# The value products of an attention kernel, as one product of 128 keys or as two of 64 on the two halves of TensorE's rows

## The chip, the cores and the metric

The kernel runs on one core of one Trainium2 chip. The metric is the device time of one execution in microseconds (us), lower is better. Engines are named as in the profile: PE is TensorE's matrix products, PEld its weight loads, DVE is VectorE, ACT ScalarE, POOL GpSimd, SP the engine that issues the transfers.

## What is computed

A layer norm, then an attention block with 32 heads of only 16 elements each, beside a gated feed-forward block that reads the same normalised input. All of it is float32.

```
x = A_x                                   # 1 x 2048 x 512
xn = layernorm(x)
q, k, v = split(xn @ A_wqkv)              # 32 heads of 16
p = softmax(q @ k^T / 4)                  # 2048 x 2048 for each head
s = (p @ v) @ A_wo
gate, up = xn @ B_w1, xn @ B_w3           # 512 -> 1792
g = silu((silu(gate) * up) @ B_w2)        # 1792 -> 512
return x + s * g
```

## The kernel before

**Stages.** A prologue of about 160 us normalises and transposes the input and makes queries, keys and values. Then comes one long stretch, to about 1625 us of the profile, in which attention and the feed-forward block run interleaved on PE. A tail of some 120 us multiplies by the output weights.

**Attention.** It works on pairs of heads. A phase is one pair of heads and one half of the 2048 queries, 32 phases in all. Four kinds of work on PE belong to the long stretch:

- `m` (line 389, `max_unit`): scores of 128 queries against 512 keys, of which DVE takes the row maxima (line 391). The maxima of the next phase are made during the present one. 2048 in all.
- `e` (line 626, `scores`): the scores again, keys on the output's partitions, of which ACT takes the exponential (line 629) into a tile `pt` of 128 keys x 512 queries. 2048 in all.
- `pv` (line 639, `values`): four exponentiated tiles times the values of their 128 keys, with a column of ones that adds up the softmax's denominator. Each of the four is a product with 17 output columns that stands on its own group of 32 columns of the array, so the four stand side by side. 512 such groups, 16 for each phase, and all 16 of a phase add up in one PSUM bank, `pv`. Operands are float32, and the hardware carries out each such product as two instructions.
- `f` (line 857, `Lanes.emit`): the products of the feed-forward block, each matrix product as three of rounded parts.

**Halves of the rows.** `m`, `e` and `f` have at most 64 rows of weights. Each stands on rows 0 to 63 of the array (lane 0) or on rows 64 to 127 (lane 1), and two of different lanes run at the same time. A `pv` product of before needs all 128 rows.

**PSUM.** Of eight banks one is `pv`. The other seven are handed out one by one by `take`, to whichever of `m`, `e`, `f` asks next. A bank that went to an `m` is free again when DVE has read it, that of an `e` when ACT has. A product of the `f` kind holds its bank while 12 to 24 instructions of each lane add up in it; two such products can be open at once, one to a lane.

**The order.** A table of letters, `ORDER_OF_ISSUE`, sets what PE gets next: small letters are lane 0, capitals lane 1, `s` stands for an `e` product, `v` for a group of value products, `r` for one behind the transposition of new maxima. An entry for which the program's own clock (`Model`) sees no bank or no input yet is put off and tried again at each later entry. The letters are counted here as they come out in the built program. There are 380 places with one or more `v` in a row, 512 groups in all. In the long stretch 214 of the ways from one such place to the next have 12 other entries or fewer; they hold 287 groups and 610 `m`. The other 141 ways are longer, 46 entries on the average; they hold 189 groups, 1331 `m` and 1333 `e`, which together are 41% of their entries.

**Taking out.** At the end of a phase `take_out` has ACT copy the bank `pv` to SBUF (line 645), and the first `pv` product of the next phase waits for that copy. Sums of exponentials then go through DRAM to become reciprocals on all partitions, and POOL multiplies. The ring of `pt` tiles has 23 buffers (`PTS`); an `e` of a new group is let out only while fewer than that are owed.

Of the kernel before, what the change touches and what calls it, by code (L numbers as in the profile page):

```python
# [9 lines left out]
F32 = mybir.dt.float32  # L10
# [7 lines left out]
P = 128  # L18
S, D, F = 2048, 512, 1792
# [19 lines left out]
AHEAD = 5  # L39
HALF = P // 2  # L40
# [105 lines left out]
def kernel(ctx: ExitStack, tc: tile.TileContext, x, wqkv, wo, w1, w3, w2, out):  # L146
# [11 lines left out]
    BANKS = 7  # L158
# [16 lines left out]
    pv = psum.tile([P, 512], F32, tag="pv", name="pv", bufs=1)  # L175
# [242 lines left out]
    with tc.tile_pool(name="pro", bufs=1) as pro, tc.tile_pool(name="pros", bufs=1) as pros:  # L418
# [121 lines left out]
        nc.vector.memset(pv, 0.0)  # L540
# [93 lines left out]
    def values(p, half, k, pts):  # L634

        last = (p, half) == LAST
        for j, pt in enumerate(pts):
            key = k * 2 % NT + j // 2 if last else k
            nc.tensor.matmul(pv[32 * j:32 * j + VW, :], vt[2 * p // GH][:, key, 2 * p % GH + j % 2, :], pt,  # L639
                             start=key < 2 if last else k == 0, stop=key >= NT - 2 if last else k == NT - 1)  # L640

    def take_out(p, half):

        ot = work.tile([P, 512], F32, tag="ot", name="ot", bufs=2)
        nc.scalar.copy(ot, pv)
# [395 lines left out]
    def pt_tile(dtype):  # L1041
        return work.tile([P, 512], dtype, tag="pt", name="pt", bufs=PTS)
# [5 lines left out]
    def projecting():  # L1048

        if not steps or min(free_at) > mod.now + EARLY or not can(*steps[0][:2]):  # L1050
            return False
        what, b, t = steps.pop(0)
# [49 lines left out]
    count = {"S": 0, "M": 64, "V": 0, "chunks": 0, "phase": 1}  # L1102
# [90 lines left out]

    def issue_v():
# [4 lines left out]
        values(p, half, k, [c["pts"][j] for j in range(4)])  # L1199
# [7 lines left out]
        if k == NT - 1 and j < PHASES - 3:  # L1207
            g = take_out(p, half)
            next(g)
            outs.append([mod.now + 2.0, g, j, -1])  # L1210
        elif k == (NT - 1 if j < PHASES - 1 else NT // 2 - 1) and j >= PHASES - 3:
            sums[j] = [work.tile([P, 512], F32, tag="ot", name="ot", bufs=2)]
            nc.scalar.copy(sums[j][0], pv)
        else:
            return
        pv_free = mod.work("act", begins + mod.VALUES + 0.3, 0.6) + mod.NOTICE
# [3 lines left out]
    def half_issued(what, h):  # L1220

        if what == "f":
# [64 lines left out]

    ot, oh, ol = pt_tile(F32), pt_tile(F32R), pt_tile(F32R)
    nc.scalar.copy(ot, pv)
# [51 lines left out]
```

## Time and profile before

| | |
|---|---|
| time, two runs | 1749.95 and 1750.27 us, median 1750.11 |
| span of the profiled execution | 1747.2 us, first to last instruction |
| granted TensorE clock | 1.000 |
| PE, PEld busy | 1737.2, 1027.4 us |
| DVE, ACT, POOL busy | 1432.9, 1258.9, 764.1 us |

The profile is of one execution; its own time is known by its span, and the runs' median is 2.9 us more than that. Instruction lines such as L639 are lines of the kernel before. In the changed kernel the same statements stand a little lower: `m` at L391, its maximum at L393, `e` at L629, `pv` at L643, `f` at L867. The PE time of a row counts from an instruction's start to its modelled end, so products that follow each other at full rate overlap in it.

### The profile page before, as it was taken

The page shows a single profiled execution, that of the slowest core. Times are in us where ns is not written, and L with a number is a line of the kernel's source. Part 1 is how long each engine was busy: PE and PEld are TensorE (multiplying, and loading weights), DVE is VectorE, ACT ScalarE, POOL GpSimd, SP SyncE. Part 2 cuts the span into 40 slices and gives each one's busy share as a digit, 9 for nine tenths or more (in the row PEclk, how much of TensorE's full clock was granted, in tenths as well). Part 3 has the DMA queues.
Part 4 walks back from the last instruction along what each step waited for, and adds up shares of the span by engine and source line. Part 5 has one row for each costly group of instructions (what it writes and reads, how often), then busy time and mean ns, then how long its engine had stood idle before and what let it go on. Part 6 is the DMA issues. An engine that isn't in the chain of part 4 may idle for free.

```text
span 1747.2 us, 35524 instructions
## 1 busy us (share of the span) xinstructions
PE 1737.2 (99%) x13188; PEld 1027.4 (59%) x13188; DVE 1432.9 (82%) x2343; ACT 1258.9 (72%) x2440; POOL 764.1 (44%) x791
## 2 busy tenths in 40 slices
PE   9999999999999999999999999999999999999998
PEld 7876655555555555555555565565555565555455
DVE  7576988888888888898888888898888897898625
ACT  4223788778878787778778877788787867868861
POOL 3102744346526561546356452555265615562101
PEclk9999999999999999999999999999999999999999
DMA  8657213132323222231433231132322321331542
GB/s 286 239 200 206 59 41 71 47 71 54 80 76 85 65 56 50 62 81 47 93 98 68 51 80 29 50 68 75 101 80 62 81 39 55 101 93 31 172 155 97
DMA packets 146798, 155.37 MB, mean 89 GB/s; under 512 B 42304, under 2 KB 100672, under 8 KB 143648
## 3 DMA queue, kind: packets, MB, share of 16 engines
q1 hardware_dynamic: 145760, 151.52, 32.0%
q8 instruction: 104, 1.70, 0.4%
q10 hardware_dynamic: 864, 1.57, 0.2%
q14 instruction: 70, 0.57, 0.1%
HBM read 107.97 MB, written 44.02 MB: 87 GB/s over the span
## 4 chain that ended last, share of the span: by engine, by line
PE 92%; issue 4%; DMA 2%; SPq 1%; DVE 0%; ACT 0%; POOL 0%; ACTq 0%; POOLq 0%
PE f L857 27%; PE pv L639 26%; PE e L626 17%; PE m L389 14%; PE m L507 2%; PE e L195 2%; PE e L199 2%; PE e L197 2%; PE m L480 0%; PE m L404 0%; DMA ovl<-o 0%; DMA wl<-g 0%; SPq L894 0%; DMA inh<-in_A_x_dram 0%; DMA last<-in_A_wo_dram 0%
## 5 line engine op out<-in xcount | busy, mean ns | idle before, releaser
L391 DVE TENSOR_REDUCE mp<-m 128x1 f32<-128x512 f32 x2048 | 1301.3, 684 | 192.2 <-PE m L389 123.8
L629 ACT ACTIVATE pt<-e 128x512 f32<-128x512 f32 x2048 | 1091.3, 605 | 301.9 <-PE m L389 130.7
L626 PE MATMUL e<-qs,ks 64*128 64x512 f32 x2048 | 713.2, 413 | 1.8 <-DMA qs<-ml 1.8
L389 PE MATMUL m<-ks,qs 62*128 62x512 f32 x2048 | 691.9, 411 | 0.2 <-DVE mp L391 0.2
L639 PE MATMUL pv<-pt,vt 128*17 128x512 f32 x4096 | 515.0, 597 | 0.0
L626 PEld LDWEIGHTS e<-qs,ks 64*128 64x128 f32 x2048 | 340.1, 184 | 266.8 <-ACT pt L629 87.9
L389 PEld LDWEIGHTS m<-ks,qs 62*128 62x128 f32 x2048 | 337.1, 184 | 123.3 <-ACT pt L629 39.6
L639 PEld LDWEIGHTS pv<-pt,vt 128*17 128x17 f32 x4096 | 81.1, 96 | 202.6 <-issue 194.3
L857 PE MATMUL f<-xtl,wh 64*128 64x512 f32 x488 | 171.8, 391 | 0.0
L857 PE MATMUL f<-xth,wl 64*128 64x512 f32 x488 | 171.7, 396 | 0.0
L857 PE MATMUL f<-xth,wh 64*128 64x512 f32 x488 | 169.0, 392 | 0.0
L742 POOL TENSOR_TENSOR h<-g,h 128x512 f32<-128x512 f32 x56 | 71.9, 1284 | 215.9 <-ACT h L738 215.8
L857 PE MATMUL f<-wh,hs 64*128 64x512 f32 x496 | 148.4, 395 | 0.0
L857 PE MATMUL f<-xth,xel 64*128 64x512 f32 x408 | 147.4, 396 | 0.0
L857 PE MATMUL f<-xth,xeh 64*128 64x512 f32 x408 | 144.7, 393 | 0.0
L857 PE MATMUL f<-xtl,xeh 64*128 64x512 f32 x408 | 143.9, 392 | 0.0
L322 POOL TENSOR_TENSOR wl<-wr,wh 128x512 fp32r<-128x512 f32 x92 | 118.4, 1287 | 7.7
L857 PE MATMUL f<-xeh,hs 64*128 64x512 f32 x400 | 121.5, 393 | 0.0
L321 POOL TENSOR_SCALAR wh<-wr 128x512 fp32r<-128x512 f32 x92 | 56.9, 619 | 115.1 <-PE m L389 47.7
L322 POOL TENSOR_TENSOR xel<-wr,xeh 128x512 fp32r<-128x512 f32 x76 | 97.9, 1288 | 6.3
L726 POOL TENSOR_SCALAR th<-th 128x512 f32<-128x512 f32 x56 | 34.6, 618 | 133.2 <-ACT th L719 133.2
L857 PEld LDWEIGHTS f<-xtl,wh 64*128 64x128 f32 x488 | 85.9, 185 | 6.8
(179 smaller groups left out, 2027.4 us busy)
## 6 DMA issues: line engine op xcount, KB each, us to landing
wr<-in_B_w_dram SPq DMA_DIRECT2D x168, 256.0 KB
qs<-qk SPq DMA_DIRECT2D x186, 64.0 KB
ks<-qk SPq DMA_DIRECT2D x90, 128.0 KB
qk<-sh SPq DMA_DIRECT2D x32, 256.0 KB
qk<-sl SPq DMA_DIRECT2D x32, 256.0 KB
v<-vrow SPq DMA_DIRECT2D x16, 272.0 KB
xin<-in_A_x_dram SPq DMA_DIRECT2D x16, 256.0 KB
g<-part SPq DMA_DIRECT2D x16, 256.0 KB
```

The source lines that it names most:

```text
L195: nc.tensor.matmul(ps, lhs[1], rhs[0], start=first, stop=False)
L197: nc.tensor.matmul(ps, lhs[0], rhs[1], start=False, stop=False)
L199: nc.tensor.matmul(ps, lhs[0], rhs[0], start=False, stop=last)
L321: nc.gpsimd.tensor_scalar(hi, t, 1.0, 1.0, op0=ALU.mult, op1=ALU.mult)
L322: nc.gpsimd.tensor_sub(lo, t, raw(hi))
L389: nc.tensor.matmul(ps, qs[p % 2][64 * h:64 * h + KM, q0:q0 + P], ks[p % 2][64 * h:64 * h + KM, c * 512:(c + 1) * 512], start=True, stop=True)
L391: nc.vector.reduce_max(mp[p, half][:, h, qt, c:c + 1], ps, axis=AX.X)
L626: nc.tensor.matmul(ps, ks[p % 2][64 * h:64 * h + KR, k * P:(k + 1) * P], qs[p % 2][64 * h:64 * h + KR, q0:q0 + 512], start=True, stop=True)
L629: nc.scalar.activation(pt, ps, AF.Exp, scale=DH ** -0.5)
L639: nc.tensor.matmul(pv[32 * j:32 * j + VW, :], vt[2 * p // GH][:, key, 2 * p % GH + j % 2, :], pt, start=key < 2 if last else k == 0, stop= ...
L742: nc.gpsimd.tensor_mul(h2, g, h2)
L857: nc.tensor.matmul(ps, left[r], right[r], start=starts and lane == 0, stop=ends and lane == 1)
```

## The change

- `values` gets a lane. The keys of a `pt` tile are halved: the first 64 are multiplied on lane 0 and add up in one PSUM bank, the last 64 on lane 1 and add up in a second bank. Instead of four products of 128 rows x 17 columns there are twice four of 64 rows x 17 columns.
- The first half is issued where the group was issued before. The second half is put in a list and issued `SHIFT = 6` entries of the table later, or earlier where a next group, the end of a phase (or half of the last one), or an output product comes first.
- There are now two `pv` banks and six instead of seven for everything else.
- Taking out (`taken`) is ACT's copy of the first bank and an addition of the second on DVE; `Model` books DVE's share too.
- A new exponential is let out by the count of second halves issued (`W`), not of first ones.

In the built program 186 of the 512 groups have the two halves next to each other; in the other 326 entries lie between, five of them in 305 cases.

```diff
+SHIFT = 6
...
-    BANKS = 7
+    BANKS = 6
...
-    pv = psum.tile([P, 512], F32, tag="pv", name="pv", bufs=1)
+    pvs = [psum.tile([P, 512], F32, tag=f"pv{h}", name="pv", bufs=1) for h in range(2)]
+    pv = pvs[0]
...
-    def values(p, half, k, pts):
+    def values(p, half, k, pts, lane):
 
         last = (p, half) == LAST
+        r = slice(HALF * lane, HALF * lane + HALF)
         for j, pt in enumerate(pts):
             key = k * 2 % NT + j // 2 if last else k
-            nc.tensor.matmul(pv[32 * j:32 * j + VW, :], vt[2 * p // GH][:, key, 2 * p % GH + j % 2, :], pt,
-                             start=key < 2 if last else k == 0, stop=key >= NT - 2 if last else k == NT - 1)
+            nc.tensor.matmul(pvs[lane][32 * j:32 * j + VW, :], vt[2 * p // GH][r, key, 2 * p % GH + j % 2, :],
+                             pt[r], start=key < 2 if last else k == 0,
+                             stop=key >= NT - 2 if last else k == NT - 1)
+
+    def taken(ot):
+
+        nc.scalar.copy(ot, pvs[0])
+        nc.vector.tensor_add(ot, ot, pvs[1])
...
-        if 4 * count["V"] + PTS <= count["S"]:
+        if 4 * count["W"] + PTS <= count["S"]:
...
+    halves = []
+
+    def second_half(now=True):
+
+        for e in list(halves):
+            e[0] -= 1
+            if now or e[0] <= 0:
+                halves.remove(e)
+                values(*e[1:], 1)
+                count["W"] += 1
+
     def issue_v():
...
-        values(p, half, k, [c["pts"][j] for j in range(4)])
+        second_half()
+        pts = [c["pts"][j] for j in range(4)]
+        values(p, half, k, pts, 0)
+        halves.append([SHIFT, p, half, k, pts])
+        if k in (NT - 1, NT // 2 - 1):
+            second_half()
...
-        pv_free = mod.work("act", begins + mod.VALUES + 0.3, 0.6) + mod.NOTICE
+        pv_free = mod.work("dve", mod.work("act", begins + mod.VALUES + 0.3, 0.6), 0.6) + mod.NOTICE
...
     def half_issued(what, h):
 
+        second_half(False)
```

**PE, at a place where one group follows another closely** (near 541.5 us of the profile; `pt` numbers name the exponentiated tiles, pv_65 is the first bank, pv_66 the second). Before:

```order
L389 MATMUL m_7617<-ks0_134,qs0_132 128x512
L626 MATMUL e_7620<-qs1_133,ks1_135 128x512
L639 MATMUL pv_65<-pt_7519,vt_1710 17x512
L639 MATMUL pv_65<-pt_7563,vt_1710 17x512
L639 MATMUL pv_65<-pt_7527,vt_1710 17x512
L639 MATMUL pv_65<-pt_7573,vt_1710 17x512
L626 MATMUL e_7631<-qs1_133,ks1_135 128x512
L389 MATMUL m_7635<-ks0_134,qs0_132 128x512
L626 MATMUL e_7642<-qs1_133,ks1_135 128x512
L389 MATMUL m_7646<-ks0_134,qs0_132 128x512
L626 MATMUL e_7649<-qs1_133,ks1_135 128x512
L626 MATMUL e_7653<-qs1_133,ks1_135 128x512
```

The same place in the changed kernel:

```order
L643 MATMUL pv_65<-pt_8008,vt_1712 17x512
L643 MATMUL pv_65<-pt_8062,vt_1712 17x512
L629 MATMUL e_8124<-qs1_134,ks1_136 128x512
L391 MATMUL m_8128<-ks0_135,qs0_133 128x512
L629 MATMUL e_8131<-qs1_134,ks1_136 128x512
L391 MATMUL m_8135<-ks0_135,qs0_133 128x512
L629 MATMUL e_8138<-qs1_134,ks1_136 128x512
L643 MATMUL pv_66<-pt_8000,vt_1712 17x512
L643 MATMUL pv_66<-pt_8052,vt_1712 17x512
L643 MATMUL pv_66<-pt_8008,vt_1712 17x512
L643 MATMUL pv_66<-pt_8062,vt_1712 17x512
L629 MATMUL e_8146<-qs1_134,ks1_136 128x512
```

The four products became four on the first half (two of them shown) and four of the same tiles on the second half, behind five entries. The five, `SmSmS` in the table's letters, are the same as before and in the same order: lanes 1, 0, 1, 0, 1.

**PE, away from the value products** (near 1307.6 us). The `f` with wl5 and wh5 and the `e` behind them are lane 0; the `f` with wl4 and wh4 behind that `e` are lane 1. Before:

```order
L857 MATMUL f_19392<-xth_18481,xeh_1564 128x512
L857 MATMUL f_19642<-xth_18481,wl5_19023 128x512
L857 MATMUL f_19642<-xtl_18482,wh5_19022 128x512
L626 MATMUL e_19645<-qs1_133,ks1_135 128x512
L857 MATMUL f_19557<-xth_18481,wl4_19019 128x512
L857 MATMUL f_19557<-xtl_18482,wh4_19018 128x512
L389 MATMUL m_19651<-ks0_134,qs0_132 128x512
```

In the changed kernel:

```order
L867 MATMUL f_20897<-xth_19921,xeh_1566 128x512
L867 MATMUL f_21167<-xth_19921,wl5_20495 128x512
L867 MATMUL f_21167<-xtl_19922,wh5_20494 128x512
L867 MATMUL f_21078<-xth_19921,wl4_20491 128x512
L867 MATMUL f_21078<-xtl_19922,wh4_20490 128x512
L629 MATMUL e_21172<-qs1_134,ks1_136 128x512
L391 MATMUL m_21176<-ks0_135,qs0_133 128x512
```

Only a neighbour's place moved here (the `e` went behind two `f`): away from the groups the change reaches the order through the number of banks alone.

**DVE, around the end of a phase** (the maxima are L391 before and L393 after). Before:

```order
L408 TENSOR_TENSOR ml<-m,mh 16x128
L391 TENSOR_REDUCE mp<-m 128x1 x43
L653 RECIPROCAL rec<-sums 128x16
L391 TENSOR_REDUCE mp<-m 128x1 x13
L397 TENSOR_REDUCE mx<-mp 128x16
```

In the changed kernel:

```order
L410 TENSOR_TENSOR ml<-m,mh 16x128
L393 TENSOR_REDUCE mp<-m 128x1 x18
L650 TENSOR_TENSOR ot<-ot,pv 128x512
L393 TENSOR_REDUCE mp<-m 128x1 x23
L663 RECIPROCAL rec<-sums 128x16
L393 TENSOR_REDUCE mp<-m 128x1 x15
```

The addition of the second bank stands in the row of maxima, 18 of them behind the row `ml`; the maxima behind it wait until ACT's copy and the addition are done.

More of the change, by code (lines that the diff above doesn't have):

```diff
@@ L539 @@
             run(products)
-        nc.vector.memset(pv, 0.0)
+        for t in pvs:
+            nc.vector.memset(t, 0.0)
         for n in range(2):
@@ L1101 @@
     opened, closed = [], []
-    count = {"S": 0, "M": 64, "V": 0, "chunks": 0, "phase": 1}
+    count = {"S": 0, "M": 64, "V": 0, "W": 0, "chunks": 0, "phase": 1}
     keys = {0: 0.0, 1: 0.0}
@@ L1212, in issue_v @@
             sums[j] = [work.tile([P, 512], F32, tag="ot", name="ot", bufs=2)]
-            nc.scalar.copy(sums[j][0], pv)
+            taken(sums[j][0])
         else:
             return
-        pv_free = mod.work("act", begins + mod.VALUES + 0.3, 0.6) + mod.NOTICE
+        pv_free = mod.work("dve", mod.work("act", begins + mod.VALUES + 0.3, 0.6), 0.6) + mod.NOTICE
         if j in sums:
@@ L1286 @@
                 mod.wait(0.1)
+    second_half()
     ot, oh, ol = pt_tile(F32), pt_tile(F32R), pt_tile(F32R)
-    nc.scalar.copy(ot, pv)
+    taken(ot)
     def whole(adder):
```

3 lines of the change are left out of this document (2 added, 1 removed).

## The prediction, as put on record before the result

> **What bounds the kernel now.** I read the page's first parts, then the long stretch as a window, then the timeline around one group of value products, then two places that show when the array has to run empty.
>
> ```profile
> span 1747.2 us, 35524 instructions
> PE 1737.2 (99%) x13188; PEld 1027.4 (59%) x13188; DVE 1432.9 (82%) x2343; ACT 1258.9 (72%) x2440; POOL 764.1 (44%) x791
> ...
> PE f L857 27%; PE pv L639 26%; PE e L626 17%; PE m L389 14%; PE m L507 2%; PE e L195 2%; PE e L199 2%; PE e L197 2%; PE m L480 0%; PE m L404 0%; DMA ovl<-o 0%; DMA wl<-g 0%; SPq L894 0%; DMA inh<-in_A_x_dram 0%; DMA last<-in_A_wo_dram 0%
> ...
> L391 DVE TENSOR_REDUCE mp<-m 128x1 f32<-128x512 f32 x2048 | 1301.3, 684 | 192.2 <-PE m L389 123.8
> L629 ACT ACTIVATE pt<-e 128x512 f32<-128x512 f32 x2048 | 1091.3, 605 | 301.9 <-PE m L389 130.7
> ```
>
> ```profile
> 160.00:1625.00 1465.00, 1462.95 (x11782) 841.44 (x11784) 1269.05 (x2063) 1148.59 (x2218) 720.36 (x737) 1.00 0.28 69
> ```
>
> PE is busy 99% of the span and is 92% of the chain of waits, a quarter of it in the value products. In the window of the long stretch (columns: length, then busy PE, PEld, DVE, ACT, POOL) PE fills 1463 of 1465 us, but DVE has 1269 and ACT 1149. So PE is the bound, with DVE 13% behind it. A busy PE is not a full array, though, and the timeline of all engines at one group shows where it isn't:
>
> ```profile
> 541.45 0.39 PE L626 MATMUL e<-qs,ks 64*128 64x512 f32 x1
> 541.76 0.13 PEld L639 LDWEIGHTS pv<-pt,vt 128*17 128x17 f32 x8 [0.36 <-issue]
> 541.77 1.05 PE L639 MATMUL pv<-pt,vt 128*17 128x512 f32 x8
> 542.75 0.18 PEld L626 LDWEIGHTS e<-qs,ks 64*128 64x128 f32 x1 [0.85 <-ACT pt L629]
> 542.75 0.49 PE L626 MATMUL e<-qs,ks 64*128 64x512 f32 x1
> 542.75 0.49 PE L389 MATMUL m<-ks,qs 62*128 62x512 f32 x1
> 543.08 0.39 PE L626 MATMUL e<-qs,ks 64*128 64x512 f32 x1
> 543.28 2.06 ACT L629 ACTIVATE pt<-e 128x512 f32<-128x512 f32 x4 [0.69 <-PE m L389]
> 543.31 0.39 PE L626 MATMUL e<-qs,ks 64*128 64x512 f32 x2
> 543.31 1.29 DVE L391 TENSOR_REDUCE mp<-m 128x1 f32<-128x512 f32 x2 [0.26 <-PE m L389]
> 543.64 1.05 PE L639 MATMUL pv<-pt,vt 128*17 128x512 f32 x8
> ```
>
> The chain of waits gives a group's length:
>
> ```profile
> 1453.55 1.84 PE pv L639 x16
> ...
> 1462.74 0.99 PE pv L639 x8
> ```
>
> One more group costs 1.84 - 0.99 = 0.85 us. From 543.08 to 543.31 a pair of entries takes 0.23. The last `e` before the group starts at 541.45, so its lane is free at 541.68, but the group starts at 541.77: 0.09 lost. The group's 0.85 ends at 542.62, the next pair starts at 542.75: 0.13 lost. The pair after that comes 0.33 later instead of 0.23: 0.10 lost. Together **0.32 us around each place with value products**, and the group's weights (541.76) are loaded only as it starts.
>
> **Does the change remove that?** It does if a change of the number of columns needs no emptying, and if the lanes run on independently. For the first, PE alone where products of 128 rows meet products of 62, all of 128 columns:
>
> ```profile
> 106.43 0.39 PE L199 MATMUL e<-xeh,wqh 128*128 128x512 f32 x1
> 106.75 0.73 PE L389 MATMUL m<-ks,qs 62*128 62x512 f32 x4
> 107.41 0.50 PE L507 MATMUL m<-wqh,xel 128*128 128x512 f32 x1
> 107.75 0.39 PE L507 MATMUL m<-wql,xeh 128*128 128x512 f32 x1
> ```
>
> and the timeline where 128 columns turn to 16 at unchanged 128 rows:
>
> ```profile
> 154.83 0.39 PE L199 MATMUL e<-xth,wqh 128*128 128x512 f32 x1
> 154.83 0.09 PEld L404 LDWEIGHTS m<-ident,nm 128*16 128x16 f32 x1
> 155.06 0.27 PE L404 MATMUL m<-ident,nm 128*16 128x128 f32 x1
> 155.06 0.19 PEld L195 LDWEIGHTS e<-xth,wql 128*128 128x128 f32 x1
> 155.08 0.47 PE L195 MATMUL e<-xth,wql 128*128 128x512 f32 x1
> ```
>
> In the first, 0.32 (106.43 to 106.75) and 0.34 (107.41 to 107.75) stand in place of 0.23: the row halving alone costs what the groups cost. In the second, the weights of 16 columns load under the product before (154.83), and their product starts 0.23 later, at full rate. So I read the loss as one of the row division; the changed groups keep to the 64 rows of their neighbours. The Trainium skill ("TensorEngine Tiling (Array Packing)", Key Properties) says that changing the tiling mode drains TensorE, and counts 64x128 and 64x32 as different modes; the trace agrees for rows and not for columns at 128 rows, and has no row for columns at 64.
>
> For the second, PE at a place where the order of issue (shown with the change) has a lane-0 `e` ahead of two lane-1 `f` with wl and wh:
>
> ```profile
> 1307.58 0.60 PE L857 MATMUL f<-xth,wl 64*128 64x512 f32 x2
> 1307.89 0.53 PE L857 MATMUL f<-xtl,wh 64*128 64x512 f32 x2
> 1308.12 0.39 PE L626 MATMUL e<-qs,ks 64*128 64x512 f32 x1
> ```
>
> All four `f`, those two included, have started before the `e`. A lane does pass instructions of the other that are stuck. In the trace it passes two or three; a changed group leaves eight and more.
>
> **The sum, against the span of 1747.2.** In the changed kernel each half group takes its lane 0.85 us, so a lane's work is what it was, and with 2.5 slots of 0.23 between the halves the lanes stay level.
>
> 1. *Losses around the groups*: 380 places x 0.32 = -122 us. Ends: nothing (no overlap), and all of it.
> 2. *DVE in the close groups.* From 541.77 to 543.64, 1.87 us, stand a group and six entries, three of them maxima. On PE they would take 0.85 + 3 x 0.23 = 1.54. DVE needs (row of two maxima: 1.29 - 0.68 = 0.61 apart) 3 x 0.61 = 1.83. So here 0.04 is saved instead of 0.32. Taking the larger of the two needs for each of the 214 short ways, by their letters in the order of issue, about half of 214 x 0.32 = 68 us stays: +35.
> 3. *A bank fewer.* An `e` and an `m` start at 542.75; ACT begins at 543.28 and takes 0.60, DVE begins at 543.31 and takes 0.68, so a bank is held 1.13 to 1.24 us, 1.2 on the average, where nothing queues. While two `f` products are open, `m` and `e` have five banks of seven now, and four of six then: at most 4 / 1.2 = 3.3 a microsecond instead of 4.2. On the long ways they are 41% of the entries, two entries per 0.23 us: 3.6 a microsecond between groups, and 18.9 per way. 18.9 / 3.3 = 5.7 us is under the 6.35 that PE would take (1.34 groups x 0.85 + 22.7 pairs x 0.23), but not always evenly spread. Ends: 0, and all of the 141 x 0.32 = 45 or more (third rival). I take half: +22.
> 4. *Taking out*: 32 additions on DVE of about 0.6 us = +19 at most, where DVE is what PE waits for. DVE then waits for ACT's copy with maxima queued behind it, and the first group's second half of the next phase waits for the addition; six entries cover that (0.7 us). I count 19; ends 0 and 32 x 1.3 = 42, if ACT's 0.6 is uncovered too.
> 5. *At nothing*: 4096 more instructions on PE, with as many loads (eight loads take 0.13 us at 541.76, under the other lane's work; uncovered 512 x 0.13 = 67); `pt` tiles released up to a microsecond later (the ring of 23 holds nearly six groups; uncovered, ACT waits that microsecond at some groups); the reciprocal's transfers a DVE step later, with entries of the next phase over them; no transfer is issued in another place, so the queues of SP and POOL change only with what releases them. The prologue is as before, PE bound at 128 rows.
>
> -122 + 35 + 22 + 19 = -46: a span of 1701, and with the 2.9 us between span and median **1704**; for entries that wait a little for each other at 326 split groups (0.01 each) I say 1708. That is 2.4% less. About 2% either way, 35 us, is what a measurement of this kernel can tell from no change.
>
> **The rivals.**
>
> *All of it arrives.* Banks and additions stay hidden: 1747 - 122 + 35 = 1660, 1663 as a time; without DVE's share too 1628. For it speaks that no wait for a bank is seen outside the 0.85 of a group. Against it: DVE at 1269 + 19 in about 1360 us would be 95% busy.
>
> *The queue blocks (slower).* If an entry of lane 0 behind the first half holds up lane 1 behind it, a split group takes 0.85 + 2.5 x 0.23 + 0.85, less 0.23 beside the second half and 0.12 beside the first (a capital leads in half the cases) = 1.93, where 0.85 + 0.32 + 0.58 = 1.75 stood: 326 x 0.18 = +59; the some 55 places without a split save 18; with the additions 1747 + 59 - 18 + 19 = 1807, **1810**. It decides where fewer than about eight stuck instructions can be passed. The Trainium skill ("TensorE: Matmul & The Clock Gate", What overlaps and what doesn't) has matmuls start in strict program order; at 1307.89 to 1308.12 the trace differs.
>
> *The array empties for columns too, so the change doesn't do what it says.* Each split group then has two turns of 0.85 + 0.32 instead of one: 326 x 1.17 = +381, 2147 with the additions, **2150**. Against it are the rows at 154.83 to 155.08. By the skill's rule on modes, above, this is what would happen.
>
> *Banks become the bound (slower).* On the long ways four banks and 18.9 results in 6.69 us (1.34 x 0.85 + 0.32 + 22.7 x 0.23) break even at a hold of 4 x 6.69 / 18.9 = 1.42 us; at 1.24 they don't bind. If entries that start under a half group hold their bank for its 0.85 us, some three of 18.9, the mean is 1.2 + 3 x 0.85 / 18.9 = 1.33; with a queue of 0.2 on DVE it is 1.5, a way takes 7.1, and 141 x 0.4 = 56 us are lost: 1747 + 56 + 19 = 1822, **1825**, or near 1750 at 1.42.
>
> **The numbers.** My forecast, 1708, has a chance of 0.42, with a range of its own of 1675 to 1750; 0.27 of that lies below 1715. All of it arriving: 0.17. Banks binding: 0.20, half of it within 2%. The blocked queue: 0.13, nearly all slower. The emptied array: 0.08. So faster by over 2%: 0.27 + 0.17 = 0.44; slower: 0.10 + 0.12 + 0.08 = 0.30; within: 0.26. A range of 1640 to 1825 leaves out the emptied array and the ends of the others.
>
> **What would show it.** Right: `pv` rows of 64 x 17 with other rows' products starting inside their 0.85 us; a weight load for them ahead of their start; the next entry of the other lane 0.23 behind its predecessor. DVE's share of the long stretch rises to some 93%. Wrong: no product of lane 1 starts within a first half (blocked or emptied; emptied if 0.09 and more is lost at each end of every half); waits of PEld on ACT and DVE outside the groups, with PE rows apart (banks). Step 2 is wrong if close groups come every 1.6 us, step 4 if DVE idles 1 us ahead of each L650.

## The result and the profile after

The changed kernel takes 2308.41 us (two runs, 2306.80 and 2310.03) where the kernel before takes 1750.11: 1.3194 times as long (95% interval 1.3155 to 1.3232), 558 us slower. The prediction was 1708 with a range of 1640 to 1825. The profiled execution after has a span of 2305.0 us, 557.8 more than before, at a granted clock of 0.997.

Parts of the page of the changed kernel (span, PE, the chain of waits by line, and two groups of instructions):

```profile
span 2305.0 us, 43733 instructions
...
PE 2286.0 (99%) x17284; PEld 1107.5 (48%) x17284; DVE 1481.3 (64%) x2377; ACT 1307.2 (57%) x2440; POOL 763.1 (33%) x791
...
PE pv L643 33%; PE f L867 21%; PE e L629 18%; PE m L391 15%; PE m L509 2%; ACT pt L632 1%; PE e L197 1%; PE e L201 1%; PE e L199 1%; DVE mp L393 1%; PE m L406 0%; DMA qk<-sl 0%; PE m L482 0%; DMA inh<-in_A_x_dram 0%; PE pv L452 0%
...
L393 DVE TENSOR_REDUCE mp<-m 128x1 f32<-128x512 f32 x2048 | 1328.2, 686 | 639.0 <-PE m L391 431.3
L643 PE MATMUL pv<-pt,vt 64*17 64x512 f32 x8192 | 840.3, 595 | 0.0
```

PE still counts as busy for 99% of the span, although it does the same work in 558 us more: a time in which one lane works and the other stands still counts in full. What shows the loss is the other side: DVE's maxima have hardly grown (1301 to 1328 us), but DVE stood idle ahead of them for 639 us where it was 192, most of it for PE, and the value products' share of the chain went from 26% to 33%.

The window of the long stretch of the changed kernel (length, then busy PE, PEld, DVE, ACT, POOL):

```profile
160.00:2180.00 2020.00, 2008.35 (x15712) 922.87 (x15710) 1324.86 (x2110) 1205.53 (x2235) 722.35 (x740) 1.00 0.21 51
```

It answers to 1465 us before, with about the same work of DVE, ACT and POOL in it. DVE's share fell from 87% to 66%; the prediction had it rise to 93%.

The timeline around two groups of the changed kernel, PE and its weight loads:

```profile
699.68 0.39 PE L867 MATMUL f<-xth,xel 64*128 64x512 f32 x1
699.68 0.63 PE L391 MATMUL m<-ks,qs 62*128 62x512 f32 x2
...
700.24 0.13 PEld L643 LDWEIGHTS pv<-pt,vt 64*17 64x17 f32 x8 [0.37 <-issue]
700.24 1.05 PE L643 MATMUL pv<-pt,vt 64*17 64x512 f32 x8
701.22 0.18 PEld L867 LDWEIGHTS f<-xtl,xeh 64*128 64x128 f32 x1 [0.85 <-issue]
701.22 0.50 PE L867 MATMUL f<-xtl,xeh 64*128 64x512 f32 x1
...
701.23 0.73 PE L391 MATMUL m<-ks,qs 62*128 62x512 f32 x2
...
701.89 1.93 PE L643 MATMUL pv<-pt,vt 64*17 64x512 f32 x32
...
703.75 0.49 PE L391 MATMUL m<-ks,qs 62*128 62x512 f32 x1
```

The eight instructions at 700.24 are one half of a group, on one lane. They load their weights only as they start, no product of the other lane begins beside them, and the next loads and products begin together 0.98 us later. Before, a whole group took 0.98 from its start to the next product's (541.77 to 542.75). So **half a group alone costs what a whole group cost**. The 32 instructions at 701.89 are two groups with their halves side by side: 1.86 us, about as much as two groups before (1.84).

Cutting the long stretch, in both traces, at each start of value products and at each next start of another product (160 us to the last `f`; the sums are worked out from PE's starts, the entries of each lane are counted in the built program, and 0.205 is what is lost ahead of a place and in the second pair behind it):

| part of the long stretch, us | before | after | more |
|---|---|---|---|
| places with value products (361; 655) | 453.6 | 744.5 | 291 |
| ends of the stretches between: 0.205 x 355 and 649 | 73 | 133 | 60 |
| the fuller lane of each stretch, entries x 0.227 | 895 | 961 | 66 |
| what is left of the stretches: waits | 28 | 150 | 122 |

That is 539 us; the other 19 lie in the tail. The first three lines belong together: the array runs empty at 655 places instead of 361, and with five entries between two halves one lane has three of them and the other two. The fourth, the waits, is another thing.

### The profile page after: what moved, and what is told of

Read it like the earlier page. It is cut to its first block, busy times and chain, and to the rows that moved or that the text cites. A ratio compares the mean times of both kernels' runs of the same rounds, so it can differ in the third digit from the quotient of the medians.

```text
span 2305.0 us, 43733 instructions
## 1 busy us (share of the span) xinstructions
PE 2286.0 (99%) x17284; PEld 1107.5 (48%) x17284; DVE 1481.3 (64%) x2377; ACT 1307.2 (57%) x2440; POOL 763.1 (33%) x791
## 4 chain that ended last, share of the span: by engine, by line
PE 92%; issue 4%; ACT 1%; DVE 1%; SPq 1%; DMA 1%; POOL 0%; ACTq 0%; POOLq 0%; DVEq 0%
PE pv L643 33%; PE f L867 21%; PE e L629 18%; PE m L391 15%; PE m L509 2%; ACT pt L632 1%; PE e L197 1%; PE e L201 1%; PE e L199 1%; DVE mp L393 1%; PE m L406 0%; DMA qk<-sl 0%; PE m L482 0%; DMA inh<-in_A_x_dram 0%; PE pv L452 0%
## 5 line engine op out<-in xcount | busy, mean ns | idle before, releaser
L393 DVE TENSOR_REDUCE mp<-m 128x1 f32<-128x512 f32 x2048 | 1328.2, 686 | 639.0 <-PE m L391 431.3
L632 ACT ACTIVATE pt<-e 128x512 f32<-128x512 f32 x2048 | 1133.7, 598 | 762.1 <-PE e L629 390.5
L643 PE MATMUL pv<-pt,vt 64*17 64x512 f32 x8192 | 840.3, 595 | 0.0
L629 PE MATMUL e<-qs,ks 64*128 64x512 f32 x2048 | 789.0, 440 | 5.7 <-ACT pt L632 2.4
L391 PE MATMUL m<-ks,qs 62*128 62x512 f32 x2048 | 766.5, 433 | 5.4 <-ACT pt L632 3.6
L391 PEld LDWEIGHTS m<-ks,qs 62*128 62x128 f32 x2048 | 343.4, 185 | 269.1 <-ACT pt L632 109.1
L643 PEld LDWEIGHTS pv<-pt,vt 64*17 64x17 f32 x8192 | 124.5, 92 | 286.7 <-issue 280.1
L867 PE MATMUL f<-xtl,wh 64*128 64x512 f32 x488 | 184.8, 413 | 0.0
L867 PE MATMUL f<-xth,wl 64*128 64x512 f32 x488 | 183.9, 411 | 0.0
L867 PE MATMUL f<-xth,wh 64*128 64x512 f32 x488 | 180.7, 407 | 0.0
L867 PE MATMUL f<-wh,hs 64*128 64x512 f32 x496 | 160.1, 408 | 0.5 <-ACT pt L632 0.5
```

Source lines behind the costliest of these rows:

```text
L391: nc.tensor.matmul(ps, qs[p % 2][64 * h:64 * h + KM, q0:q0 + P], ks[p % 2][64 * h:64 * h + KM, c * 512:(c + 1) * 512], start=True, stop=True)
L393: nc.vector.reduce_max(mp[p, half][:, h, qt, c:c + 1], ps, axis=AX.X)
L629: nc.tensor.matmul(ps, ks[p % 2][64 * h:64 * h + KR, k * P:(k + 1) * P], qs[p % 2][64 * h:64 * h + KR, q0:q0 + 512], start=True, stop=True)
L632: nc.scalar.activation(pt, ps, AF.Exp, scale=DH ** -0.5)
L643: nc.tensor.matmul(pvs[lane][32 * j:32 * j + VW, :], vt[2 * p // GH][r, key, 2 * p % GH + j % 2, :], pt[r], start=key < 2 if last else k == 0,
L867: nc.tensor.matmul(ps, left[r], right[r], start=starts and lane == 0, stop=ends and lane == 1)
```

## The experiments

Times stand against the kernel before, timed beside each of them (medians 1749.9 to 1750.3), with the ratio and its 95% interval where a kernel was timed more than once.

**What makes the array run empty.** Products of constants, one kind at a time, in a row of six pairs of rounded products of 64 rows x 128 columns:

```
for _ in range(4):
    c = bank("c", "lowA")
    nc.tensor.matmul(c[0:17], w[low, 0:17], m[low], start=True, stop=True)
    lanes("afterA")
```

> This kernel leaves out the whole computation: it runs matrix products of constants on PE alone, four times each, and the output is a constant. Between six pairs of products of 64 rows x 128 columns (the two halves of the rows) one product on lane 0 is put: A four-byte float of 17 columns at column 0, B the same at column 32, C of rounded type with 16 columns, D four-byte float of 128 columns, E rounded with 64, F rounded with 100, G the four groups of 17 side by side. Then the same among products of 128 rows: H rounded with 16 columns, I float with 17, J float with 128, K a transposition to 16 columns, L float with 17 at column 32. Theory 'columns empty the array': A, B and G start only when both lanes are done, some 0.1 us late, their weights are loaded as they start, and the next pair starts 0.1 us and more behind their end; D has its weights loaded ahead and the other lane goes on beside it; C, E and F tell from how few columns on it happens (C as A). Among 128 rows H, I and L lose 0.2 to 0.3 us each and K nothing, since a transposition is not split by columns. Theory 'the type empties the array' (four-byte float among rounded): A, B, D, G, I, J, L lose, C, E, F, H do not. Theory of the prediction, rows alone: nothing in A to L loses 0.1 us.

> As the first run of single products, nothing of the layer is computed: among pairs of rounded products of 64 rows x 128 columns one product is put on lane 0, four times each: four-byte float with A 16, B 32, C 64, D 100 columns; rounded with E 128 and F 32 columns; G four-byte float with 17 columns on both lanes; H rounded with 16 columns on both lanes. What a product adds to its six pairs (6 x 0.2275) is compared with its own time (0.85 us float, 0.23 rounded). In the first run it was 0.33 more for float with 17 columns, at 64 and at 128 rows, 0.11 more for rounded with 16 to 100 columns, 0.02 more for float with 128. Theory 'columns and type together': A to C lose 0.33, D 0.1 or less, E nothing, F 0.11, G 0.33 once for both, H 0.11. Theory 'one product on one lane costs 0.11 of evenness whatever its shape, and only 32 columns or fewer empty the array': E 0.11 too, H nothing, C and D as E, A and B 0.33.

The timeline of the first of these kernels at a float product of 17 columns (lowA, one product on lane 0):

```profile
20.12 0.39 PE L41 MATMUL afterA<-mr,wr 64*128 64x512 f32 x1
20.13 0.39 PE L42 MATMUL afterA<-mr,wr 64*128 64x512 f32 x1
20.44 0.11 PEld L52 LDWEIGHTS lowA<-m,w 64*17 64x17 f32 x2 [0.36 <-issue]
20.44 1.03 PE L52 MATMUL lowA<-m,w 64*17 64x512 f32 x2
21.40 0.18 PEld L41 LDWEIGHTS afterA<-mr,wr 64*128 64x128 f32 x1 [0.85 <-PE afterA L42]
21.40 0.49 PE L41 MATMUL afterA<-mr,wr 64*128 64x512 f32 x1
```

PE alone in the second kernel, at a float product of 64 columns (lowC) and at one of 100 (lowD):

```profile
40.24 0.39 PE L41 MATMUL afterC<-mr,wr 64*128 64x512 f32 x1
40.57 1.07 PE L60 MATMUL lowC<-m,w 64*64 64x512 f32 x2
41.57 0.50 PE L41 MATMUL afterC<-mr,wr 64*128 64x512 f32 x1
...
48.00 0.39 PE L42 MATMUL afterC<-mr,wr 64*128 64x512 f32 x1
48.23 0.59 PE L64 MATMUL lowD<-m,w 64*100 64x512 f32 x1
48.48 0.50 PE L42 MATMUL afterD<-mr,wr 64*128 64x512 f32 x1
48.65 0.59 PE L64 MATMUL lowD<-m,w 64*100 64x512 f32 x1
48.68 0.80 PE L41 MATMUL afterD<-mr,wr 64*128 64x512 f32 x1
```

The first shows the pattern of the changed kernel with nothing else around it: 0.32 to its start where pairs follow each other by 0.23, then 0.96, weights loaded late at both ends. The 100 columns start 0.23 behind their neighbour, and the other lane's product starts at 48.48 in their midst. From 64 to 100 columns the loss goes. PE alone in the first kernel, among products of 128 rows, at a float product of 17 columns (wholeI) and at a transposition of floats to 16 (wholeK):

```profile
91.70 1.03 PE L86 MATMUL wholeI<-m,w 128*17 128x512 f32 x2
92.66 1.65 PE L47 MATMUL afterI<-mr,wr 128*128 128x512 f32 x6
94.24 1.03 PE L86 MATMUL wholeI<-m,w 128*17 128x512 f32 x2
...
105.91 1.66 PE L47 MATMUL afterK<-mr,wr 128*128 128x512 f32 x6
107.41 0.27 PE L94 MATMUL wholeK<-ident,w 128*16 128x128 f32 x1
107.63 1.66 PE L47 MATMUL afterK<-mr,wr 128*128 128x512 f32 x6
```

The float product and its six neighbours take 2.54 us (91.70 to 94.24), which is 0.33 more than 0.85 and six times 0.2275; the transposition and its six take 1.72 (105.91 to 107.63), 0.13 more than 0.22 and six times 0.2275. Over all kinds, what a product adds to six pairs (or six products of 128 rows) beyond its own time:

| the product put in | us more |
|---|---|
| float, 16, 17, 32 columns on 64 rows, 17 on 128; 17 also at column 32 | 0.33 to 0.34 |
| float, 64 columns | 0.37 |
| four of 17 columns side by side; one of 17 on each lane | 0.35; 0.34 |
| float, 100 and 128 columns | 0.02 to 0.03 |
| rounded, 16, 32, 64, 100 and 128 columns, on 64 rows; 16 on 128 | 0.11 to 0.12 |
| transposition of floats to 16 columns, 128 rows (beyond the 0.22 to the next start) | 0.13 |

The 0.11 of the rounded kind is the same for 16 columns as for 128, so it is none of the columns; in the profile the next pair's weights wait there for the last product in the same bank, which is this kernel's own wait. Rounded products of 16 columns start 0.23 behind their neighbours, without a gap. So it is neither the columns alone nor the type alone: **float products of few columns make the array run empty: on 64 rows those of 16 to 64, on 128 rows that of 17**. The first theory of the first run was right on A, B, G, D, I, L and K, and wrong on C and H. Of the second run's theories the first was right on all but E, the rounded product of 128 columns, which was to lose nothing and shows the 0.11 of its kind.

**The changed kernel with products that are not divided by columns.** `values` makes one product of 64 rows x 128 columns (of ones) in each half in place of four of 17, reading one of the four tiles; the value products of all phases but the last are left out.

```diff
+        if not last:
+            nc.tensor.matmul(pvs[lane], ones[r], pts[3][r], start=k == 0, stop=k == NT - 1)
+            return
```

> The changed kernel, but each half of a group is one product of 64 rows x 128 columns (of ones, four-byte float, two instructions of 0.43 us, so the same 0.85 us of its lane) in place of four of 17 columns. It leaves out the value products of all phases but the last; everything else, the order, the banks and the additions are the changed kernel's. Theory 'columns empty the array': without a division of the columns the halves run beside the other lane, so the time falls from 2308 to what the prediction said of the changed kernel, 1660 to 1750. Theory 'the type empties the array': about 2300 as before. Theory 'the order blocks' (a lane cannot pass stuck instructions of the other): the halves start with loaded weights, but no product of lane 1 starts within a first half, some 1810 to 2000.

1930.72 us, timed once. PE in this kernel, where such halves lie among entries:

```profile
704.36 0.49 PE L631 MATMUL e<-qs,ks 64*128 64x512 f32 x1
704.36 0.69 PE L644 MATMUL pv<-pt,ones 64*128 64x512 f32 x1
704.69 0.39 PE L631 MATMUL e<-qs,ks 64*128 64x512 f32 x1
704.89 0.59 PE L644 MATMUL pv<-pt,ones 64*128 64x512 f32 x1
704.92 0.80 PE L393 MATMUL m<-ks,qs 62*128 62x512 f32 x1
```

Here `e` and `m` of the other lane do start beside a half, so the lanes run on by themselves as the prediction has it. The time lies in the range of the third theory (1810 to 2000), but the sign that this theory names, that nothing of the other lane starts within a half, isn't there; the first theory had the sign and missed the time. With the columns out of the way the kernel is still 180 us slower than before. Something else in the change costs more than the halves could bring.

**One bank fewer, alone**, and **the change with nothing between the halves**:

```diff
-    BANKS = 7
+    BANKS = 6
```

> The kernel before with six banks for m, e and f in place of seven, and nothing else. Theory 'the bank costs little' (the prediction's third term is +22 for the changed kernel): 1750 to 1775. Theory 'banks bind' (the prediction's fourth rival): 1800 and more.

```diff
         halves.append([SHIFT, p, half, k, pts])
-        if k in (NT - 1, NT // 2 - 1):
-            second_half()
+        second_half()
```

> The changed kernel with the second half issued right behind the first in every group. So there are as many places with value products as before, the two halves lie side by side, and what is left of the change is one bank fewer, the additions and 4096 more instructions. Theory 'each place is a turn of the array, and the halves apart doubled the places': both halves together take what a whole group took, 0.98 to 1.01 us from start to the next product's start, and the time is the kernel before's plus the bank and the additions, 1750 to 1800. If banks, additions or the number of instructions carry a large part of the 558 us, it stays over 1900.

The kernel before with six banks takes 1987.93 us (1.1361, 1.1342 to 1.1380): **238 us for one bank**, as the theory of binding banks has it. The order is not what costs: in the two built programs all but some ten of the 8640 `m`, `e`, `f` and groups come out in the same places of the order. With the halves side by side the change takes 2006.15 (1.1465, 1.1448 to 1.1482), 18 more than that. Both halves take 1.006 us, against 0.983 of a whole group, which is 9 of the 18 at 362 places; the rest is about what the additions can be. So the theory of 1750 to 1800 was right on the halves and wrong on the time, and the bank makes up the difference. The view of waits counts the idle time ahead of PE's weight loads by what ended it, here a reader of a bank (us in all, times, longest). In the kernel before:

```profile
PEld e L626 <- ACT pt L629: 87.9, 110, 0.9
PEld e L626 <- DVE mp L391: 83.1, 100, 2.2
PEld m L389 <- ACT pt L629: 39.6, 52, 0.9
PEld m L389 <- DVE mp L391: 30.8, 50, 0.9
```

The same groups with six banks:

```profile
PEld e L626 <- DVE mp L391: 154.1, 261, 0.9
PEld e L626 <- ACT pt L629: 146.2, 347, 0.9
PEld m L389 <- ACT pt L629: 100.1, 227, 0.9
PEld m L389 <- DVE mp L391: 74.1, 164, 0.9
```

241 us became 474. Not all of it is waiting: a load right behind value products counts the 0.85 us in which they have the array. Sorted by the load ahead, that part is 229 of the 241 us before and 221 of the 474 with six banks. What is left grew from 13 us (43 times) to 253 (739 times), 241 more, which is the 238. A single one of them, in the timeline of the kernel with six banks:

```profile
541.74 1.09 ACT L629 ACTIVATE pt<-e 128x512 f32<-128x512 f32 x2 [0.18 <-PE e L626]
...
542.01 0.39 PE L857 MATMUL f<-xel,hs 64*128 64x512 f32 x1
542.02 0.40 PE L389 MATMUL m<-ks,qs 62*128 62x512 f32 x1
542.39 0.18 PEld L626 LDWEIGHTS e<-qs,ks 64*128 64x128 f32 x1 [0.41 <-ACT pt L629]
542.39 0.50 PE L626 MATMUL e<-qs,ks 64*128 64x512 f32 x1
...
542.40 0.50 PE L857 MATMUL f<-xel,hs 64*128 64x512 f32 x1
```

ACT ends its first exponential at 542.3; the `e` at 542.39 needs that bank. The `f` of the other lane at 542.40, which in the trace has no wait of its own, is held up behind it: 0.38 from 542.01 to 542.39 in place of 0.23. A wait for a bank stops both lanes here, where an entry that waited only for its own lane was passed (the prediction's row at 1308.12).

**The turns alone.** The kernel before, seven banks, all 128 rows, but a group's four products issued as two and, where the change issues its second half, the other two (the lines of `values` that divide the group; the one bank `pv` and `BANKS = 7` are back as before):

```diff
         for j, pt in enumerate(pts):
+            if j // 2 != lane:
+                continue
```

> The kernel before (seven banks, one bank for the value products, no addition, all 128 rows), but a group's four products are issued as two and, up to six entries of the table later, two: the same entries as in the changed kernel lie between, and places with value products become as many as there. Two products side by side take the 0.85 us that four take. So this doubles the turns and changes nothing else. Theory 'the turns and the bank are two losses that each stand alone': from the trace of the changed kernel, 655 places in place of 361 (744 us against 454) give +291, the loss at the ends of the stretches between +60, the odd number of entries between that one lane has to take alone +66: 1750 + 417 = 2167, with few waits for banks. The prediction's third rival, without its additions, gives 2131. If the changed kernel's time is mainly the bank's, it stays under 2000.

2165.73 us (1.2374, 1.2355 to 1.2392), on the number. Its trace has 653 places, 281 us more in them instead of 291, 60 and 66 as expected, and waits no longer than before; some 13 us more in the tail make up for the 10. **The same with six banks:**

> The kernel with doubled turns by columns (2166 us), with six banks in place of seven. It differs from the changed kernel (2308) only in what is halved (the four products into two and two of 128 rows, not the rows into 64 and 64) and in the missing second bank and addition. Theory 'turns and banks are all of it, and the halving of the rows brings nothing': 2280 to 2300, that is the changed kernel less some 20 for the additions. If the halves of the rows let the other lane run at least in part, the changed kernel would be faster than this one: 2320 and more.

2288.10 (1.3077, 1.3057 to 1.3096), as expected. With these the result is built up step by step: 1750 + 416 (twice the turns) + 122 (a bank fewer) + 20 (the second bank, the additions, the halves of the rows) = 2308. The bank costs 122 here and 238 where the turns are not doubled. A reading that fits is that readers catch up and banks come free while the array has a half group to itself. How much of the 122 comes from the plan was not tried: `Model` books the array's time once for a group, also where the group has two places. And halving the rows brings nothing that can be seen: the kernel that halves by columns on all 128 rows is 20 us faster, about what the second bank and its additions cost with the halves side by side (18).

**An even number of entries between the halves** (`SHIFT = 7`):

> The changed kernel with a distance of seven entries of the table in place of six, so that six entries lie between the halves, as many to one lane as to the other, and the 136 places at which one entry stood between a second half and the next first half now have the two side by side. In the built program 562 places instead of 695. Theory 'every place costs a turn': 66 us of uneven lanes go, and some 133 places of 0.98 us with 0.2 us at the end of the stretch ahead of each, about 155 us: 2308 - 66 - 155 = 2087; some of it comes back as waits for banks, up to 2150. If the distance between the halves mattered by itself (more instructions than the queue can pass), it would stay near 2300.

2170.91 (1.2414, 1.2393 to 1.2435): faster than the change by 137, but 84 short of the expected and 21 above the 2150 that was left open. In its trace 64 us of uneven lanes went and 129 us of places and stretch ends, a little less than the 66 and 155 expected; waits grew from 150 to 211, more than was left open.

**Fewer places than before.** The kernel before, with a group held back until two can go together:

> The kernel before, but a group is held back until the next one is due and the two are issued together, so that the ways between places become 273 in place of 383 in the built program. Nothing else is changed (seven banks, 128 rows). Theory 'a place costs 0.32 us': 110 x 0.32 = 35 us less, 1715. Against it: the exponentiated tiles of a held group are owed for longer, and the ring of 23 lets fewer new exponentials out; and longer stretches without a group leave the banks no time to come free. By the bank's measured price the second could cost more than it saves: 1715 to 1800.

1836.57 (1.0494, 1.0479 to 1.0510), slower than any of the times expected. In the trace the places went from 361 to 238 and saved 13 us in themselves and 24 at the stretch ends, but the waits in the longer stretches grew from 28 to about 147. Most of that is banks: weight loads that waited for a reader, not counting those behind value products, went from 13 us to 107. So a place with value products is not only a loss; it is also the time in which banks come free, and 0.32 x the number of places was never all to be had.

**Why a bank is that dear.** Maxima over 128 keys of 512, with six banks and with seven (the edit's main line; the exponential's factor goes with it):

```diff
-        nc.vector.reduce_max(mp[p, half][:, h, qt, c:c + 1], ps, axis=AX.X)
+        nc.vector.reduce_max(mp[p, half][:, h, qt, c:c + 1], ps[:, :P], axis=AX.X)
```

> The kernel before with six banks, and DVE takes each maximum over 128 of the 512 keys only, so that it gives the bank of an m back some 0.4 us sooner (the exponential's factor is made smaller so that nothing overflows). It leaves out three quarters of the maxima; products, order and banks are those of the run with six banks, 1988 us. Theory 'a bank is missing while its reader is still at work': the mean hold falls from 1.37 to some 0.9 us for an m, with less queueing for an e, about as much as the seventh bank was worth, so the time comes back by 150 us or more, to 1750 to 1835. Theory 'the order that six banks lead to is what costs': it stays above 1930.

> The same shortening of the maxima in the kernel before itself, with seven banks. It leaves out three quarters of the maxima. It bounds what waits for banks and for DVE cost the kernel before: after the 0.2 us at the end of each stretch, its trace has 28 us of such waits in the long stretch. So 1720 to 1750 if those go; much less than 1720 would mean that DVE or the banks bound the kernel before in a way that its waits do not show.

With seven banks: 1747.61 (0.9987, 0.9978 to 0.9997). Neither DVE nor the maxima's banks bound the kernel before. With six: 1945.45 (1.1119, 1.1102 to 1.1136), 42 less than 1988. That is a miss for the first theory and within what the second allows (above 1930), but the order that the second speaks of is all but the same with six banks as with seven, so it is not the cause either. An `m` now held its bank for 0.78 us in place of 1.37, an `e` as long as ever (1.25). One place in the timeline of this kernel:

```profile
543.14 0.62 PE L389 MATMUL m<-ks,qs 62*128 62x512 f32 x2
543.36 0.49 DVE L391 TENSOR_REDUCE mp<-m 128x1 f32<-128x128 f32 x2 [2.01 <-PE m L389]
543.39 1.08 ACT L629 ACTIVATE pt<-e 128x512 f32<-128x512 f32 x2 [1.93 <-PE m L389]
...
544.03 0.18 PEld L626 LDWEIGHTS e<-qs,ks 64*128 64x128 f32 x1 [0.71 <-ACT pt L629]
```

Two maxima are done by 543.85, the first of them well before; the `e` at 544.03 waits for ACT all the same. Which bank a product gets is settled when the program is built, by the plan's own clock, and that still gave a maximum 0.605 us. Two more runs tell the plan's part; the first tells it of the shorter maxima:

```diff
-        COST = {"act": 0.495, "dve": 0.605}
+        COST = {"act": 0.495, "dve": 0.2}
```

> As the run with six banks and shortened maxima (1945 us; three quarters of the maxima left out), but the program's own clock, by which banks are handed out, is told of it: 0.2 us for a maximum in place of 0.605. Theory 'a product waits, in order, for the one bank that the plan gave it': the shortened maxima brought only 42 us because the plan went on giving out banks as if an m held its bank for long, so that e products waited for banks that ACT still read while those of m products lay free (in that run's profile an e waits 0.71 us for ACT at 544.03, when a maximum had ended at 543.65). Told of it, the time falls by another 60 us or more, to 1885 or less. Theory 'ACT's reading alone limits': it stays within 20 us of 1945.

1854.63 (1.0600, 1.0582 to 1.0617): 91 less from a number in the plan, with every instruction's work unchanged and all but some ten of the 8640 in the same order. What the number changes then is which bank each of them gets. So a product waits in order for one named bank, and a plan that is wrong about the hold makes it the wrong one. The second puts an entry off until a bank is near:

```diff
-        return min(free_at) <= mod.now + EARLY
+        return min(free_at) <= mod.now + 0.2
...
-        return any(left[h] for _, left in rooms)
+        return any(left[h] for _, left in rooms) and min(free_at) <= mod.now + 0.2
```

> The kernel before with six banks, and an e or an m is put off until the program's own clock sees a bank within 0.2 us; before, an e was let out 0.5 us ahead of its bank and an m without regard to banks. The built program has 440 places with value products in place of 388 (some 52 x 0.32 = 17 us more) and lanes less even (29 us more). Theory 'the waits in order could be filled by feed-forward products': the waits of 231 us shrink by half or more, 1988 - 115 + 46 = 1920 or less. Theory 'there is nothing to fill them with, the banks' number is the bound': 1988 + 46 = 2034 or more.

1959.96 (1.1200, 1.1183 to 1.1217), between the two theories. The waits fell from 259 to 187 us, all of it in the ways of 12 entries or fewer (0.65 to 0.27 us each beyond PE's time, the 0.2 at a stretch's end included; the longer ways stayed at 1.4), and more places and uneven lanes took 45 back. So waits in order were a part that other entries could fill; for the long ways they could not. Of the 238 us, 133 are shown to hang on how long an `m` holds its bank together with the plan; the other 104 (1854.63 against 1750.15) stay open. That an `e` holds its bank for ACT's 0.6 is the likely cause, and was not tried.

None of the kernels that compute the whole layer was faster than the one before.

## Why the prediction was wrong

**The step that failed first** is "a change of the number of columns needs no emptying". The row behind it, 154.83 to 155.08 of the kernel before, was read rightly but was a row of another thing: line 404 is a transposition, and the runs show that a transposition of floats to 16 columns does not empty the array (0.13, about as the rounded products, and its weights load ahead), while a product of floats with 17 columns on the same 128 rows does (0.33). The Trainium skill ("TensorEngine Tiling (Array Packing)", Restrictions) says that column tiling disables the transpose mode for float inputs; by that the line would not be a product on a divided array, and these runs agree (0.13 against 0.33). The rule that the prediction set against its row, that a change of the tiling mode drains TensorE (the Trainium skill, the same page, Key Properties), was right for float products: from 128 columns to 17 on the same 64 rows and back costs 0.33 us here. For rounded ones no such loss shows at 16 to 64 columns (0.11, as at 128). The prediction had a chance of 0.08 for the emptied array. The rows at 106.43 and 107.41 did show that halving the rows empties the array; they could not show that columns don't.

**Term 1**, -122, became +416 (the kernel with doubled turns). The rival of the emptied array had the mechanism and its shape (0.09 and more lost at each end of every half) and +381 as its price. It was mis-sized in two ways: it multiplied 326 by 1.17 = 381, where the trace has 294 more places at 0.98 + 0.21, 351 together (the table's first two lines); and it left out that an odd number of entries makes the lanes uneven, 66. That its 2150 lies near the 2166 of the doubled turns is in part luck: the two misses have opposite signs, and it counted additions that this kernel doesn't have. Its other miss was to let the bank cost nothing beside it.

**Term 3**, a bank fewer, +22 with an upper end of 45 (56 as a rival), measured 238 alone and 122 beside the doubled turns. It went wrong in four places. It took the hold of a bank from one place, 1.2 us, where nothing queued; over the long stretch of the same trace an `m` held its bank for 1.42 us on the average and an `e` for 1.28. With 1.35 four banks need 18.9 x 1.35 / 4 = 6.4 us for a long way, no longer less than the 6.35 that PE takes. It counted the groups' 1.34 x 0.85 us in full as time in which four banks serve products; readers go on then, but no `m` or `e` starts, and without that time PE needs only 22.7 x 0.23 = 5.2 us, less than the prediction's own 5.7. It priced the 141 long ways alone; in the trace of six banks the long ways lost 139 us and the 214 short ones 92. And it took an entry without a bank for one that is put off, as the description of the kernel says. Lines 1133 and 1153 do that for an `e`, 0.5 us ahead of its bank, and not at all for an `m`:

```
        return min(free_at) <= mod.now + EARLY
        return any(left[h] for _, left in rooms)
```

So such a product stands at the head of PE's queue, with both lanes behind it.

**Term 2** (DVE in close groups, +35) was not tested: the groups it speaks of never came closer. **Term 4** (additions, +19) and **term 5** (4096 instructions at nothing) have the right sum, in part by luck: together they are the 18 and 20 us of the two pairs of runs, but about 9 of each lie in the value products themselves (two halves side by side take 1.006 us where a whole group takes 0.983; a half of the rows alone takes 0.98 where a half of the columns takes 0.97). So term 5 is not nothing, and term 4 is some 11 at most. The prediction's own sign of a wrong step 4 did appear: DVE, whose addition takes 0.69 us, stood idle for 54 us ahead of the 33 additions, 1.6 us each. PE's loads waited for the addition 0.3 us in all, and DVE was busy for only 66% of the long stretch, so that little of this idle time can have cost.

**The lanes running on by themselves**, on which the gain was built, was right where it can be seen (704.36 to 704.92): against the halves side by side, products that don't divide the columns saved 75 us (2006 to 1931). The rival of the blocked queue was not tested in its own terms, since those halves are two instructions and not eight. But 75 us is a third of what the seventh bank is worth. Had the columns cost nothing, the change would still have been slower than the kernel before, near 1930 by that run: two of its rivals came true at once, and each of them alone would have decided it.

## What to carry to other kernels

Before a place is taken as proof that an operation doesn't make the array run empty, see that the row is of the same kind of operation: same type, same division of rows and of columns, a product and not a transposition. Price a PSUM bank by a run with one fewer, which is a change of one number, not by a mean hold; the mean leaves out that readers need the pauses, that products wait in order, and that the plan named the bank. And where a kernel loses a fixed time at each of many places, ask what else happens in that time, since doing away with the places took here (1837) more than it gave.

## What the runs showed that was not expected

- One float product of 17 columns takes the array as long as four side by side (0.96 and 0.98 us to the next product), and two of them on the two lanes as long as one.
- The loss of 0.33 us goes with float products of 64 columns or fewer (0.37 at 64). It was absent at 100 columns, and with rounded products even at 16; why the rounded ones differ was not settled.
- One bank of eight is worth 238 us in a kernel whose weight loads wait for banks 13 us in all, the idle time behind value products aside. How long a kernel waits for banks doesn't tell what one fewer would cost.
